# Attention tiles 0 to 7 of a two-layer kernel: exponentials per head, queries and keys loaded in 2 KB pieces and turned by products

## Chip, cores and metric

The kernel runs on one core of one Trainium2 chip. The metric is device time in microseconds (us) of one execution, the median of 3 runs. TensorE is called PE below, VectorE DVE, ScalarE ACT, GpSimd POOL and SyncE SP, as in the profile.

## What is computed

```python
def _attn_ref(q, k, v):                 # B, H, S, D = 8, 8, 576, 64; chunks of 64 tokens
    scores = scale * np.matmul(q_c, k_c.transpose(0, 1, 2, 4, 3))     # scale = 1/8
    scores = scores - np.max(scores, axis=-1, keepdims=True)
    attn = np.exp(scores)
    attn = attn / (np.sum(attn, axis=-1, keepdims=True) + 1e-09)
    return np.matmul(attn, v_c).reshape(B, H, S, D)

def reference(...):
    x = attn_out.transpose(0, 2, 1, 3).reshape(4608, 512)
    h = x @ w_in1;  g = np.maximum(h, 0.0) + alpha * np.minimum(h, 0.0);  x = g @ w_out1
    h = x @ w_in2;  g = h - np.tanh(h);                                  return g @ w_out2
```

Attention is within chunks of 64 tokens. q, k and v are float32; the weights (512x2048 and 2048x512 twice) and alpha are float64 and reach the chip as 64-bit words.

## The kernel before

The 4608 tokens are 36 tiles of 128 (two chunks, all 8 heads). Nine blocks of 512 tokens (4 tiles) go through layer 1, then through layer 2. A layer's hidden width of 2048 is walked in 16 pieces f of 128: `up` (L447) makes h of one f and 512 tokens with 12 products on PE, `act_g` (L461) applies the activation on ACT and DVE, `down` (L504) adds 12 products into four accumulators. Every float32 operand is held as a high and a low part, hence three products for one.

The program writes out the order of each engine's work itself: an engine runs its instructions in the order in which the functions are called. Tiles 0 to 3 are prepared before any step (L673 to L766). Tiles 4 to 7 are prepared inside steps 0 to 7 (`step_first`, L785), a step being one f of the first two blocks; while these run, the weights are converted from 64-bit words on ACT and DVE, one home d a step.

One tile's way, in the early form that the change touches:

- `load_natural` (L229) brings q and k of the tile, tokens on partitions: 1024 pieces of 256 bytes each, issued on SP.
- `att_a_early` (L280) turns q (i = 0) or k (i = 1) with four PE transposes of 128x128 into a PSUM tile (tr, trh) and copies it on ACT (on DVE for tile 0 and for k of tile 2) into qt or kt.
- `att_s_early` (L327) makes the scores, 16 products of 64x64, in PSUM: in `first_banks` for tiles 0 to 3, whose halves alternate (`first_banks[:, t % 2]`), in sc afterwards.
- `att_e` (L344) takes the maximum of each head's row on DVE (mx, L348), subtracts it there from all 512 columns into SBUF (p, L350), and takes the exponential of the whole tile on ACT (L353).
- `att_n` (L356) sums on DVE (sm, L359), adds 1e-9 (L361), inverts (rd, L362) and multiplies (L363, on POOL for tiles 0 to 2).
- `att_t_early` (L398) transposes p on PE (ptr) and copies it on ACT (pte or pt, L405); `att_v_early` (L407) multiplies with v (xpe or xp); `att_xh` and `att_xl` write the high part on ACT (xh, L435) and the low part on DVE (xl, L439).

`convert_a(d)` (L149) takes the raw words of weight home d apart on ACT (wm L113, wr L116), `convert_b(d, ops)` (L165) puts float32 together in four operations on DVE (ops 0 to 3: L126, L130, L132, L136), `split_w` (L183) makes the high part on ACT (L174) and the low part on DVE or POOL (L181). Homes s0 and s1 hold w_in pieces 0 and 1 of layer 1, home 0 the next two pieces; up(0) needs s0, up(1) needs s1. `warm(n)` puts n products of zeros on PE. In step 1 the transposes ptr of tile 4 stand ahead of up(1) on PE.

Of the kernel before, what the change touches and what calls it, by code (L numbers as in the profile page):

```python
# [27 lines left out]
def kernel(  # L28
# [136 lines left out]
    def convert_b(d, ops=(0, 1, 2, 3)):  # L165
        to_f32_b([w_parts[d]], ops)
# [113 lines left out]
    def att_a_early(t, i):  # L280

        if t < NPT + 2:
            tr = ps_y.tile([P, HP, P], F32, tag=f"y{i if t < NPT else 2 - 2 * (t % 2) + i}", name="tr")
        else:
            tr = ps_h.tile([P, HP, P], F32, tag="h", name="trh")
        for hp in range(HP):
            nc.tensor.transpose(tr[:, hp, :], raws[t][i][:, hp * P:(hp + 1) * P], ident)
        to = (qts, kts)[i][t].rearrange("p h c d -> p h (c d)")
        if t == 0 or (t, i) == (2, 1):
            nc.vector.tensor_copy(to, tr)  # L290
        else:
            nc.scalar.activation(out=to, in_=tr, func=AF.Copy)  # L292
# [48 lines left out]
                    )  # L341
        scs[t] = sc

    def att_e(t, early=False):  # L344
        scv = scs.pop(t)
        a, b = (HP, 2) if early else (2, HP)
        mx = stat.tile([P, a, b, 1], F32, tag="mx", name="mx")
        nc.vector.tensor_reduce(out=mx[:, :, :, 0], in_=scv, op=ALU.max, axis=AX.X)  # L348
        p = first_p[:, t] if t < NPT else att.tile([P, H, D], F32, tag="p", name="p")
        nc.vector.tensor_tensor(  # L350
            out=p.rearrange("p (a b) d -> p a b d", a=a), in0=scv, in1=mx.to_broadcast([P, a, b, D]), op=ALU.subtract
        )
        nc.scalar.activation(out=p, in_=p, func=AF.Exp, scale=scale)  # L353
        ps[t] = p

    def att_n(t, engine=nc.vector):  # L356
        p = ps[t]
        sm = stat.tile([P, H], F32, tag="sm", name="sm")
        nc.vector.tensor_reduce(out=sm, in_=p, op=ALU.add, axis=AX.X)  # L359
        rd = stat.tile([P, H, 1], F32, tag="rd", name="rd")  # L360
        nc.vector.tensor_scalar(out=sm, in0=sm, scalar1=1e-9, scalar2=None, op0=ALU.add)  # L361
        nc.vector.reciprocal(out=rd[:, :, 0], in_=sm)  # L362
        engine.tensor_tensor(out=p, in0=p, in1=rd.to_broadcast([P, H, D]), op=ALU.mult)  # L363
# [43 lines left out]
    def att_v_early(t):  # L407
        vt, pt = vts.pop(t), pts.pop(t)
        if t < NPT:
            xp = [ps_y.tile([P, HP, D], F32, tag=f"y{2 - 2 * (t % 2) + c}", name="xpe") for c in range(2)]  # L410
        else:
            both = new_banks("xp")[:, :, :HP * D].rearrange("p c (h d) -> p c h d", h=HP)
            xp = [both[:, c] for c in range(2)]
        for hp in range(HP):
            for e in range(2):
                for c in range(2):
                    r = slice(64 * c, 64 * c + 64)
                    nc.tensor.matmul(
                        out=xp[c][64 * e:64 * e + 64, hp, :],
                        lhsT=vt[r, 2 * hp + e, :],  # L420
                        rhs=pt[r, hp, 64 * e:64 * e + 64],
                        start=True,
                        stop=True,
                    )
        xps[t] = xp
# [239 lines left out]
            qts[t0 + t], kts[t0 + t] = qt[:, t], kt[:, t]  # L665

    def load_first(t):
        load_natural(t, first_raw[t // 2][:, t % 2])

    new_first(0)  # L670
    load_first(0)
# [3 lines left out]
    load_first(3)  # L675
    load_v(0)
    load_v(1)
    load_w("s1")
    load_v(2, first_v[:, 0])
    load_v(3, first_v[:, 1])  # L680
    arow = stage.tile([P, 512], F32, tag="st", name="arow")
    nc.sync.dma_start(out=arow[:KF, :P], in_=alpha.rearrange("(f p) -> f p", p=P))
    load_first(4)
    load_w(0)
    load_w(1)
    load_first(5)
    load_v(4, first_v[:, 2])
# [19 lines left out]
    att_a_early(1, 0)  # L707
    att_s_early(0)
    att_a_early(1, 1)
    att_e(0, True)  # L710
    warm(3)
    att_s_early(1)
    att_n(0, nc.gpsimd)
    convert_a("s0")
    att_a_early(2, 0)
    att_e(1, True)
    warm(4)
    att_a_early(2, 1)
    convert_b("s0", ops=(0, 1))
# [4 lines left out]
    convert_b("s0", ops=(2,))  # L724
    att_a_early(3, 0)
    att_a_early(3, 1)
    att_e(2, True)
    convert_b("s0", ops=(3,))
    warm(3)
    att_s_early(3)  # L730
# [54 lines left out]
    def step_first(step, j, t0, f, ends, x, acc):  # L785
# [133 lines left out]
```

## Time and profile before

| | |
|---|---|
| median of 3 runs | 1680.23 us (1678.89 to 1683.86) |
| the profiled execution | 1681.05 us |
| its span on the core | 1679.2 us |
| PE busy | 1651.2 us, 98% of the span |
| DVE, ACT, POOL busy | 1291.5, 817.0, 231.7 us |
| mean granted clock of PE | 0.996 |
| chain that ended last, by engine | PE 92%, DVE 3%, SP's queue 2%, DMA 1% |

How to read it: busy time is the sum of an engine's instructions. The chain that ended last is followed back from the last instruction, at each step to what released it. Windows give busy time in a stretch of the span, with the clock that PE was granted (1.00 is 2.4 GHz) and the share of time in which the DMA engines moved data. In a timeline a row is one or several like instructions with their start, their time, and the idle time of the engine before them with what ended it; a row "x32" of 16 products counts each float32 product twice.

### The profile page before, as it was taken

The page shows a single profiled execution, that of the slowest core. Times are in us where ns is not written, and L with a number is a line of the kernel's source. Part 1 is how long each engine was busy: PE and PEld are TensorE (multiplying, and loading weights), DVE is VectorE, ACT ScalarE, POOL GpSimd, SP SyncE. Part 2 cuts the span into 40 slices and gives each one's busy share as a digit, 9 for nine tenths or more (in the row PEclk, how much of TensorE's full clock was granted, in tenths as well). Part 3 has the DMA queues.
Part 4 walks back from the last instruction along what each step waited for, and adds up shares of the span by engine and source line. Part 5 has one row for each costly group of instructions (what it writes and reads, how often), then busy time and mean ns, then how long its engine had stood idle before and what let it go on. Part 6 is the DMA issues. An engine that isn't in the chain of part 4 may idle for free.

```text
span 1679.2 us, 24428 instructions
## 1 busy us (share of the span) xinstructions
PE 1651.2 (98%) x9405; PEld 1360.4 (81%) x9405; DVE 1291.5 (77%) x1864; ACT 817.0 (49%) x1465; POOL 231.7 (14%) x171
## 2 busy tenths in 40 slices
PE   7899999999999999999999999999999999999998
PEld 6688888888887888888887888888888888888886
DVE  7878855666666666564358989898989998999987
ACT  5756544454544454454445444444444444444443
POOL 1000000000000000000146222222222222222221
PEclk9999999999999999999999999999999999999999
DMA  9661424333333333431333010101010101010000
GB/s 228 192 188 40 114 52 100 95 95 86 90 84 102 87 90 70 101 95 39 113 100 114 1 51 1 51 0 51 0 51 1 51 1 51 1 41 10 20 7 26
DMA packets 215269, 112.77 MB, mean 67 GB/s; under 512 B 170592, under 2 KB 186992, under 8 KB 215152
## 3 DMA queue, kind: packets, MB, share of 16 engines
q1 hardware_dynamic: 215152, 111.20, 24.1%
q8 instruction: 74, 1.21, 0.3%
q14 instruction: 43, 0.35, 0.1%
HBM read 81.80 MB, written 29.36 MB: 66 GB/s over the span
## 4 chain that ended last, share of the span: by engine, by line
PE 92%; DVE 3%; SPq 2%; DMA 1%; issue 1%; ACT 1%; DVEq 0%; ACTq 0%
PE y L511 45%; PE hps L455 45%; PE sc L318 1%; SPq L224 1%; DVE g L501 1%; SPq L219 1%; PE sc L389 1%; DVE g L500 0%; DMA ysc<-yst 0%; DMA first<-in_k_dram 0%; SPq L99 0%; DVE g L498 0%; DVE wm L132 0%; PE tr L276 0%; DVE wm L136 0%
## 5 line engine op out<-in xcount | busy, mean ns | idle before, releaser
L455 PE MATMUL hps<-xh,w 128*128 128x512 f32 (+1 forms) x2312 | 573.3, 390 | 5.2 <-ACT kt L292 5.2
L455 PEld LDWEIGHTS hps<-xh,w 128*128 128x128 f32 x2312 | 434.2, 188 | 95.7 <-ACT kt L292 5.7
L455 PE MATMUL hps<-xl,w 128*128 128x512 f32 (+1 forms) x1156 | 309.0, 389 | 0.0
L511 PE MATMUL y<-ghi,w 128*128 128x512 f32 x1152 | 300.6, 394 | 2.7 <-ACT yst L531 2.7
L511 PE MATMUL y<-w,ghi 128*128 128x512 f32 x1152 | 293.9, 390 | 2.5 <-ACT ghi L481 2.5
L493 ACT ACTIVATE sq<-hps 128x512 f32<-128x512 f32 x144 | 86.1, 598 | 401.0 <-PE hps L455 400.5
L484 POOL TENSOR_TENSOR glo<-g,ghi 128x512 fp32r<-128x512 f32 x144 | 185.6, 1289 | 579.9 <-ACT ghi L481 579.9
L511 PEld LDWEIGHTS y<-w,ghi 128*128 128x128 f32 x1152 | 215.8, 188 | 49.0 <-ACT ghi L481 4.4
L455 PEld LDWEIGHTS hps<-xl,w 128*128 128x128 f32 x1156 | 217.5, 188 | 45.2
L511 PEld LDWEIGHTS y<-ghi,w 128*128 128x128 f32 x1152 | 213.1, 188 | 48.4 <-ACT yst L531 3.2
L469 DVE SCALAR_TENSOR_TENSOR g<-neg,nalpha_sb,g 128x512 f32<-128x512 f32 x144 | 107.4, 746 | 179.3 <-ACT g L468 179.3
L500 DVE SCALAR_TENSOR_TENSOR g<-w,g 128x512 f32<-128x512 f32 x144 | 243.4, 1690 | 0.0
L481 ACT ACTIVATE ghi<-g 128x512 fp32r<-128x512 f32 x288 | 181.5, 630 | 103.9 <-DVE g L469 86.1
L467 ACT ACTIVATE neg<-hps 128x512 f32<-128x512 f32 x144 | 85.9, 597 | 222.4 <-PE hps L455 220.9
L511 PE MATMUL y<-glo,w 128*128 128x512 f32 x576 | 164.7, 389 | 0.0
L511 PE MATMUL y<-w,glo 128*128 128x512 f32 x576 | 162.8, 389 | 0.0
L181 POOL TENSOR_TENSOR w<-wm,w 128x1024 fp32r<-128x1024 f32 (+1 forms) x18 | 42.2, 2346 | 840.5 <-ACT w L174 840.5
L484 DVE TENSOR_TENSOR glo<-g,ghi 128x512 fp32r<-128x512 f32 x144 | 108.2, 751 | 33.7 <-ACT ghi L481 32.9
L511 PEld LDWEIGHTS y<-w,glo 128*128 128x128 f32 x576 | 108.1, 188 | 22.9 <-DVE glo L484 0.4
L511 PEld LDWEIGHTS y<-glo,w 128*128 128x128 f32 x576 | 108.1, 188 | 22.4
L501 DVE SCALAR_TENSOR_TENSOR g<-sq,g 128x512 f32<-128x512 f32 x144 | 110.1, 764 | 5.0
L502 DVE COPY_PREDICATED g<-ktc,th 128x512 f32<-128x512 uint32 x144 | 108.5, 753 | 4.9
(95 smaller groups left out, 1384.0 us busy)
## 6 DMA issues: line engine op xcount, KB each, us to landing
yraw<-ysc SPq DMA_DIRECT2D x9, 1024.0 KB, 5.8
out_dram<-yst SPq DMA_DIRECT2D x36, 256.0 KB, 2.2
raww<-in_moe_w_in_dram SPq DMA_DIRECT2D x16, 512.0 KB, 6.3
v<-in_v_dram SPq DMA_DIRECT2D x32, 256.0 KB, 4.2
raww<-in_moe_w_out_dram SPq DMA_DIRECT2D x16, 512.0 KB, 6.0
rw<-in_moe_w_in_dram SPq DMA_DIRECT2D x16, 512.0 KB, 4.3
w<-mr SPq DMA_DIRECT2D x32, 256.0 KB, 2.1
rw<-in_moe_w_out_dram SPq DMA_DIRECT2D x16, 512.0 KB, 4.1
```

The lines of the kernel that those rows point to most:

```text
L181: lo_engine.tensor_tensor(out=w_[:, :, 1], in0=w, in1=w_[:, :, 0].bitcast(F32), op=ALU.subtract)
L219: nc.sync.dma_start(out=vt[off:off + n], in_=v[b, :, s:s + n, :].rearrange("h p d -> p h d"))
L455: nc.tensor.matmul(out=hp[:, cols], lhsT=w[:, a, m], rhs=x[b][:, kk, cols], start=(kk == 0 and i == 0), stop=(kk == KD - 1 and i == 2),)
L467: nc.scalar.activation(out=neg, in_=hp, func=AF.Relu, scale=-1.0)
L469: nc.vector.scalar_tensor_tensor(out=g, in0=neg, scalar=nalpha_sb[:, f:f + 1], in1=g, op0=ALU.mult, op1=ALU.add)
L481: nc.scalar.activation(out=hi, in_=g, func=AF.Copy)
L484: lo_engine.tensor_tensor(out=lo, in0=g, in1=hi.bitcast(F32), op=ALU.subtract)
L493: nc.scalar.activation(out=sq, in_=hp, func=AF.Square)
L500: nc.vector.scalar_tensor_tensor(out=g, in0=w, scalar=ce, in1=g, op0=ALU.add, op1=ALU.mult)
L501: nc.vector.scalar_tensor_tensor(out=g, in0=sq, scalar=ca, in1=g, op0=ALU.add, op1=ALU.mult)
L502: nc.vector.copy_predicated(g, mask, th)
L511: nc.tensor.matmul(out=acc[t], lhsT=lhsT, rhs=rhs, start=(f == ends[0] and i == 0), stop=(f == ends[1] and i == 2))
```

## The change

For tiles 0 to 3 and 5 to 7 (tile 4 spans two batches) q and k are loaded by `load_grouped`: a partition holds one head and one group of 8 consecutive tokens, one piece of 2 KB, so 128 pieces a load. `att_a_early` turns such a load with 16 products of 64x64 against the identity, whose results stand in PSUM by the token's place in its group; the copy to qt or kt puts tokens into order by its reading pattern. The heads of such a tile stand as 0 to 3 and 4 to 7 in the two halves of the partitions, and `att_v_early` picks its operand accordingly. Tile 4 keeps the old load and the transposes.

For tiles 0 to 7 `att_e` becomes `att_e_early`: DVE takes the maximum (L383) and multiplies its 128x8 numbers by -scale (L384); ACT then takes eight exponentials of 128x64 (L388), straight from the scores in PSUM, with the head's maximum as bias and the row sum as a second output. `att_n` finds these sums and leaves out its own.

The order changes with it. On SP the load of s1 goes behind v of tiles 2 and 3, and weights 0 go ahead of q and k of tile 4. The conversion of s1 goes behind the products with v of tile 3 (its last two operations behind xl of tile 3), and the turn of tile 4 behind up(0), inside step 0. In step 0 all four operations on the next weights come ahead of tile 4's maximum on DVE.

```diff
+    GT = 8
+    def grouped(t):
+        return t * P % S + P <= S
+    def load_grouped(t, raw):
+        b, s = divmod(t * P, S)
+        for i, src in enumerate((q, k)):
+            nc.sync.dma_start(out=raw[:, i], in_=src[b, :, s:s + P, :].rearrange("h (g j) d -> h g (j d)", j=GT))
+        raws[t] = raw[:, 0], raw[:, 1]
...
@@ att_a_early
-        for hp in range(HP):
-            nc.tensor.transpose(tr[:, hp, :], raws[t][i][:, hp * P:(hp + 1) * P], ident)
         to = (qts, kts)[i][t].rearrange("p h c d -> p h (c d)")
+        if grouped(t):
+            tr = tr.rearrange("p a b -> p (a b)").rearrange("p (j m) -> p j m", j=GT)
+            for j in range(GT):
+                for e in range(2):
+                    r = slice(D * e, D * e + D)
+                    nc.tensor.matmul(
+                        out=tr[r, j, :], lhsT=raws[t][i][r, j * D:(j + 1) * D], rhs=ident[r, r], start=True, stop=True
+                    )
+            tr, to = tr.rearrange("p j (m g) -> p m g j", m=H), to.rearrange("p h (c g j) -> p (h c) g j", c=2, j=GT)
+        else:
+            for hp in range(HP):
+                nc.tensor.transpose(tr[:, hp, :], raws[t][i][:, hp * P:(hp + 1) * P], ident)
...
+    def att_e_early(t):
+        scv = scs.pop(t).rearrange("p h c d -> p (h c) d")
+        mx = stat.tile([P, H], F32, tag="mx", name="mx")
+        nc.vector.tensor_reduce(out=mx, in_=scv, op=ALU.max, axis=AX.X)
+        nc.vector.tensor_scalar(out=mx, in0=mx, scalar1=-scale, scalar2=None, op0=ALU.mult)
+        ps[t] = p = first_p[:, t] if t < NPT else att.tile([P, H, D], F32, tag="p", name="p")
+        sums[t] = stat.tile([P, H], F32, tag="sm", name="sm")
+        for h in range(H):
+            nc.scalar.activation(
+                out=p[:, h, :], in_=scv[:, h, :], func=AF.Exp, scale=scale, bias=mx[:, h:h + 1],
+                accum_out=sums[t][:, h:h + 1],
+            )
...
     def att_n(t, engine=nc.vector):
         p = ps[t]
-        sm = stat.tile([P, H], F32, tag="sm", name="sm")
-        nc.vector.tensor_reduce(out=sm, in_=p, op=ALU.add, axis=AX.X)
+        sm = sums.pop(t, None)
+        if sm is None:
+            sm = stat.tile([P, H], F32, tag="sm", name="sm")
+            nc.vector.tensor_reduce(out=sm, in_=p, op=ALU.add, axis=AX.X)
...
@@ att_v_early
+                h = 2 * hp + e
+                half, slot = divmod(h, HP) if grouped(t) else (e, hp)
...
-                        rhs=pt[r, hp, 64 * e:64 * e + 64],
+                        rhs=pt[r, slot, 64 * half:64 * half + 64],
...
@@ loads
     load_v(1)
-    load_w("s1")
     load_v(2, first_v[:, 0])
     load_v(3, first_v[:, 1])
+    load_w("s1")
...
-    load_first(4)
     load_w(0)
+    load_first(4)
...
@@ before the steps
     att_v_early(1)
-    convert_a("s1")
     att_n(3)
...
     att_xh(2, x0, 2 * P)
-    convert_b("s1", ops=(0, 1))
     att_xl(2, x0, 2 * P)
     att_v_early(3)
+    convert_a("s1")
+    convert_b("s1", ops=(0, 1))
...
     att_xh(3, x0, 3 * P)
+    att_xl(3, x0, 3 * P)
     convert_b("s1", ops=(2, 3))
-    att_xl(3, x0, 3 * P)
     split_w("s1", nc.vector)
-    att_a_second(4)
...
@@ step_first
         if step == 0:
             hp = up(f, x, NB, slice(2 * P, NB), hp0)
+            att_a_second(t)
             att_s_early(t)
+            some((1, 2, 3))
         if even:
-            att_e(t, True)
-        some((1, 2))
+            att_e_early(t)
+        if step:
+            some((1, 2))
...
-        some((3,))
+        if step:
+            some((3,))
```

ACT's order up to the exponential of tile 4, before (in all these rows raww, wm and wr are raw words and parts of a weight home, 128x512 for s1 and 128x1024 for home 0; xpe is the product with v):

```order
L113 ACTIVATE wm<-raww 128x512
L116 ACTIVATE wr<-raww 128x512
L435 ACTIVATE xh<-xpe 128x4x64 x2
L405 ACTIVATE pte<-ptr 128x512
L435 ACTIVATE xh<-xpe 128x4x64 x4
L174 ACTIVATE w<-wm 128x512
L292 ACTIVATE qt<-tr 128x512
L292 ACTIVATE kt<-tr 128x512
L762 ACTIVATE nalpha_sb<-first 128x16
L113 ACTIVATE wm<-raww 128x1024
L116 ACTIVATE wr<-raww 128x1024
L353 ACTIVATE p<-p 128x512
```

and with the change:

```order
L444 ACTIVATE pte<-ptr 128x512
L476 ACTIVATE xh<-xpe 128x4x64 x2
L113 ACTIVATE wm<-raww 128x512
L116 ACTIVATE wr<-raww 128x512
L476 ACTIVATE xh<-xpe 128x4x64 x2
L174 ACTIVATE w<-wm 128x512
L802 ACTIVATE nalpha_sb<-first 128x16
L113 ACTIVATE wm<-raww 128x1024
L116 ACTIVATE wr<-raww 128x1024
L314 ACTIVATE qt<-tr 128x512
L314 ACTIVATE kt<-tr 128x512
L388 ACTIVATE p,sm<-sc,mx 128x64 x8
```

The exponential of 128x512 has become eight of 128x64. The words of s1 (wm, wr of 128x512) moved from between the parts xh of tiles 0 and 1 to behind those of tile 2, and the copies qt and kt of tile 4 from ahead of home 0's words to behind them.

DVE's order from the last operations on s1 to the product of tile 4, before:

```order
L136 ISA wm<-wm,wr 128x1024
L439 TENSOR_TENSOR xl<-xpe,xh 128x4x64 x2
L181 TENSOR_TENSOR w<-wm,w 128x512
L126 TENSOR_SCALAR wm<-wm 128x1024
L348 TENSOR_REDUCE mx<-sc 128x8
L350 TENSOR_TENSOR p<-sc,mx 128x512
L130 TENSOR_SCALAR wm<-wm 128x1024
L132 SCALAR_TENSOR_TENSOR wm<-raww,wm 128x1024
L359 TENSOR_REDUCE sm<-p 128x8
L361 TENSOR_SCALAR sm<-sm 128x8
L362 RECIPROCAL rd<-sm 128x8
L363 TENSOR_TENSOR p<-p,rd 128x512
```

and with the change:

```order
L132 SCALAR_TENSOR_TENSOR wm<-raww,wm 128x512
L136 ISA wm<-wm,wr 128x1024
L181 TENSOR_TENSOR w<-wm,w 128x512
L126 TENSOR_SCALAR wm<-wm 128x1024
L130 TENSOR_SCALAR wm<-wm 128x1024
L132 SCALAR_TENSOR_TENSOR wm<-raww,wm 128x1024
L136 ISA wm<-wm,wr 128x2048
L383 TENSOR_REDUCE mx<-sc 128x8
L384 TENSOR_SCALAR mx<-mx 128x8
L400 TENSOR_SCALAR sm<-sm 128x8
L401 RECIPROCAL rd<-sm 128x8
L402 TENSOR_TENSOR p<-p,rd 128x512
```

The subtraction (p<-sc,mx) and the sum (sm<-p) are gone, a scaling of mx has come. The four operations on home 0 (wm of 128x1024, the last of 128x2048) stand together ahead of tile 4's maximum; two of them stood inside the tile's chain and the last behind it.

## Rows read from the trace of the kernel before

**Rows 1.** Windows of the whole span and of 25 to 30 us; columns as named in the first row.
```profile
core 0: us, PE busy (x) PEld busy (x) DVE busy (x) ACT busy (x) POOL busy (x), PEclk, DMA share, GB/s
0.00:30.00 30.00, 25.76 (x385) 23.01 (x385) 19.69 (x43) 15.76 (x32) 5.37 (x10) 1.00 0.98 224
30.00:47.00 17.00, 9.17 (x111) 7.67 (x113) 14.66 (x21) 12.06 (x19) 0.00 (x0) 0.80 1.03 250
47.00:100.00 53.00, 46.81 (x369) 37.42 (x365) 44.60 (x64) 33.69 (x53) 0.00 (x0) 1.00 0.65 201
100.00:1679.00 1579.00, 1569.46 (x8549) 1292.29 (x8547) 1212.57 (x1738) 755.53 (x1365) 226.32 (x161) 1.00 0.21 58
...
25.00:30.00 5.00, 4.90 (x68) 4.47 (x65) 3.78 (x8) 3.46 (x10) 0.00 (x0) 1.00 0.94 308
```

**Rows 2.** Waits of PE in the first 50 us: total us, times, longest.
```profile
PE ptr L403 <- DVE p L363: 5.7, 1, 5.7
...
PE first L335 <- DVE p L350: 1.2, 2, 0.9
PE xpe L418 <- DVE xl L439: 1.1, 1, 1.1
...
PE tr L287 <- DMA first<-in_q_dram: 0.4, 1, 0.4
```

**Rows 3.** Timeline of PE, 7 to 37 us: start, us, instruction, idle before and releaser.
```profile
7.16 1.15 PE L335 MATMUL first<-kt,qt 64*64 64x64 f32 x32
...
9.92 1.15 PE L335 MATMUL first<-kt,qt 64*64 64x64 f32 x32 [0.36 <-DVE p L350]
...
14.96 1.09 PE L287 MATMUL tr<-ident,first 128*128 128x128 f32 x8
...
17.58 1.15 PE L335 MATMUL first<-kt,qt 64*64 64x64 f32 x32 [0.85 <-DVE p L350]
...
24.99 1.20 PE L455 MATMUL hps<-xh,w 128*128 128x256 f32 x8
...
29.27 0.63 PE L455 MATMUL hps<-xl,w 128*128 128x256 f32 x4
...
36.89 1.08 PE L403 MATMUL ptr<-ident,p 128*128 128x128 f32 x4 [5.66 <-DVE p L363]
```

**Rows 4.** Groups of ScalarE by shape: busy us, mean ns, idle before.
```profile
L481 ACT ACTIVATE ghi<-g 128x512 fp32r<-128x512 f32 x288 | 181.5, 630 | 103.9 <-DVE g L469 86.1 <-DVE g L502 17.9
L495 ACT ACTIVATE w<-sq,bias_sb 128x512 f32<-128x512 f32 x144 | 104.3, 724 | 0.0
...
L467 ACT ACTIVATE neg<-hps 128x512 f32<-128x512 f32 x144 | 85.9, 597 | 222.4 <-PE hps L455 220.9 <-ACT ptb L378 0.8
...
L762 ACT ACTIVATE nalpha_sb<-first 128x16 f32<-128x16 f32 x1 | 0.2, 186 | 0.0
```

**Rows 5.** Timeline of VectorE and ScalarE, 9 to 35 us.
```profile
9.08 0.69 DVE L350 TENSOR_TENSOR p<-first,mx 128x512 f32<-128x512 f32 x1
...
10.47 0.69 DVE L359 TENSOR_REDUCE sm<-p 128x8 f32<-128x512 f32 x1 [0.69 <-ACT p L353]
...
11.19 0.17 DVE L361 TENSOR_SCALAR sm<-sm 128x8 f32<-128x8 f32 x1
...
28.18 0.75 DVE L439 TENSOR_TENSOR xl<-xpe,xh 128x256 fp32r<-128x256 f32 x2
...
29.91 1.15 ACT L113 ACTIVATE wm<-raww 128x1024 f32<-128x1024 f32 x1
...
33.68 0.58 ACT L467 ACTIVATE neg<-hps 128x512 f32<-128x512 f32 x1
...
34.16 0.59 ACT L468 ACTIVATE g<-hps 128x512 f32<-128x512 f32 x1
```

**Rows 6.** Timeline of steps 2 and 3, 63 to 75 us.
```profile
63.67 1.15 PE L335 MATMUL sc<-kt,qt 64*64 64x64 f32 x32
...
69.21 0.69 DVE L363 TENSOR_TENSOR p<-p,rd 128x512 f32<-128x512 f32 x1
...
71.56 1.22 DVE L136 CUSTOM_DVE_ANT_0 wm<-wm,wr 128x2048 uint16<-128x2048 uint16 x1
...
74.49 0.73 PE L455 MATMUL hps<-xh,w 128*128 128x512 f32 x2 [2.64 <-ACT kt L292]
```

More of the change, by code (lines that the diff above doesn't have):

```diff
@@ L342, in att_s_early, with att_e @@
         scs[t] = sc
-    def att_e(t, early=False):
+    sums = {}
+    def att_e(t):
         scv = scs.pop(t)
-        a, b = (HP, 2) if early else (2, HP)
-        mx = stat.tile([P, a, b, 1], F32, tag="mx", name="mx")
+        mx = stat.tile([P, 2, HP, 1], F32, tag="mx", name="mx")
         nc.vector.tensor_reduce(out=mx[:, :, :, 0], in_=scv, op=ALU.max, axis=AX.X)
-        p = first_p[:, t] if t < NPT else att.tile([P, H, D], F32, tag="p", name="p")
+        p = att.tile([P, H, D], F32, tag="p", name="p")
         nc.vector.tensor_tensor(
-            out=p.rearrange("p (a b) d -> p a b d", a=a), in0=scv, in1=mx.to_broadcast([P, a, b, D]), op=ALU.subtract
+            out=p.rearrange("p (a b) d -> p a b d", a=2), in0=scv, in1=mx.to_broadcast([P, 2, HP, D]), op=ALU.subtract
         )
@@ L419, in att_v_early @@
                         out=xp[c][64 * e:64 * e + 64, hp, :],
-                        lhsT=vt[r, 2 * hp + e, :],
-                        rhs=pt[r, hp, 64 * e:64 * e + 64],
+                        lhsT=vt[r, h, :],
+                        rhs=pt[r, slot, 64 * half:64 * half + 64],
                         start=True,
@@ L667, in load_first @@
     def load_first(t):
-        load_natural(t, first_raw[t // 2][:, t % 2])
+        (load_grouped if grouped(t) else load_natural)(t, first_raw[t // 2][:, t % 2])
     new_first(0)
@@ L677 @@
     load_v(1)
-    load_w("s1")
     load_v(2, first_v[:, 0])
     load_v(3, first_v[:, 1])
+    load_w("s1")
     arow = stage.tile([P, 512], F32, tag="st", name="arow")
     nc.sync.dma_start(out=arow[:KF, :P], in_=alpha.rearrange("(f p) -> f p", p=P))
+    load_w(0)
     load_first(4)
-    load_w(0)
     load_w(1)
@@ L709 @@
     att_a_early(1, 1)
-    att_e(0, True)
+    att_e_early(0)
     warm(3)
@@ L715 @@
     att_a_early(2, 0)
-    att_e(1, True)
+    att_e_early(1)
     warm(4)
@@ L726 @@
     att_a_early(3, 1)
-    att_e(2, True)
+    att_e_early(2)
     convert_b("s0", ops=(3,))
@@ L735 @@
     att_v_early(0)
-    att_e(3, True)
+    att_e_early(3)
     att_t_early(2)
```

## Prediction

> **What bounds the kernel now.** I read the windows first [rows 1]. TensorE (PE) lacks 9.5 us in the 1579 behind 100 us, but 18.3 in the first 100: 4.2 up to 30 us, 7.8 from 30 to 47, 6.2 from 47 to 100. All that the change touches lies in those 100 us. What follows has no slack, so what the start gains or loses shows whole at the end.
>
> The waits of the first 50 us say who ends PE's idle time there [rows 2]: 5.7 us on VectorE's normalisation of tile 4, 1.2 on p, the subtraction of the tile before, 1.1 on xl; on a load only 0.4. So the start is a chain from engine to engine, although the DMA engines are busy all the time. The timeline gives its beat [rows 3]: the scores of tiles 0, 1 and 3 start at 7.16, 9.92 and 17.58, the first half of up(0) at 24.99; up(0) ends at 29.9, and the transposes of tile 4 (ptr), at the head of step 1, start at 36.89.
>
> One detail of these rows carries the forecast. The scores of tile 1 (9.92) and of tile 3 (17.58) are released by "DVE p L350", the subtraction of the tile before, though they write the other half of first_banks: the two halves are one tile to the dependency tracking. Whoever reads tile t's scores last releases the scores of t+1. Today that is a subtraction which ends 1.5 us behind the scores; with the change it is the last of eight exponentials.
>
> **The change part by part.**
>
> *Exponentials.* Per tile VectorE loses the subtraction (0.69) and the sum (0.69) and gains a scaling of 128x8, like the addition to sm (0.17) [rows 5]: 1.2 us less. ScalarE loses one exponential of 128x512 and gets eight of 128x64. Price of one: an activation of 128x512 out of PSUM takes 0.597, one of 128x16 takes 0.186, so 0.83 ns an element and 0.226 for 64. A bias that is read from memory costs 0.094 (724 against 630 ns) [rows 4]: 0.320. Two in a row overlap by 0.10 (33.68 for 0.58, the next at 34.16) [rows 5], so eight take 7 x 0.22 + 0.32 = 1.86 us. The row sum is a second result that no row here shows. Below: nothing, 1.86; were the bias free as well, 7 x 0.126 + 0.226 = 1.1. Above: a further shortest activation each, 8 x 0.186, makes 3.35. I take that shortest one with its overlap, 0.09 each: **E = 2.6 us**.
>
> *Turning.* Eight transposes occupy PE for 1.09, so four for 0.55; sixteen 64x64 products on two diagonal quarters, like the scores, 1.15 [rows 3]. So 0.6 more for each of 14 turns; bounds 0 and 0.6. The copies behind now read PSUM with a stride; they move as many elements, and I leave them at 0.6.
>
> *Loads.* Fourteen loads go from 1024 pieces of 256 bytes to 128 of 2 KB. On the path lies the 0.4 us of rows 2 and no more. The weights s1 go behind two loads of v, weights 0 ahead of tile 4; both are read after 30 us, issued 10 us before. The Trainium skill, DMA: Bandwidth & Descriptors, section "Specifications", gives 512 bytes as the least piece for full rate; by it the loads get faster, and the sum would be that of the second rival below.
>
> *Start.* The scores of tile 0 stand behind three turns: 3 x 0.6, less the 0.4 of load waits: **+1.4**.
>
> *Tiles 0 to 3.* On ScalarE the copy of a next turned k or q stands ahead of the exponentials. From scores to scores: scores 1.08, turn 1.08, copy 0.65, E 2.6, release 0.15 (9.77 to 9.92) make 5.55, twice; from tile 2 to 3 there are two turns, 6.6. In all 17.7 against 10.42 (7.16 to 17.58) [rows 3]: **+7.3**.
>
> *Scores of tile 3 to up(0).* Behind scores 1.1 and ptr(1) 0.6 ScalarE has pte(1) and the high part of s0, 0.6 each, so exponentials start 2.8 us on; then E; two small operations and the product 1.15; xl 0.75 [rows 5], release 0.15, products with v and ptr 1.2: 8.6 against 7.4: **+1.2**. The halves of up(0) keep their 4.9 us.
>
> *End of up(0) to ptr of tile 4.* The conversion of s1 moved behind xh(2), and the turn of tile 4 behind up(0) and, on ScalarE, behind weights 0. Counted from the end of up(0): xl of tile 3 ended 1.0 us earlier, the last two operations on s1 end at +0.45, its high part on ScalarE at +1.1, nalpha and two conversions of weights 0 (1.15 each [rows 5]) at +3.3, the copies qt and kt at +4.4, scores at +5.5. VectorE has the four operations on weights 0 ahead of the maximum (0.7, 0.7, 1.2, 1.2, from +2.35): until +6.1; maximum and scaling +7.0, E +9.6, normalisation +10.75, ptr **+10.9** against 7.0 (29.9 to 36.89): **+3.9**. Work that lay in the tile's gaps now lies ahead of it.
>
> *Steps 1 to 6.* Here VectorE is the beat: from scores (63.67) to the product (69.21), to wm (71.56), then kt on ScalarE and up at 74.49 [rows 6]. The exponentials can start 2.1 us behind the scores and end at 4.7, the sum is gone, and the product ends at 5.8 instead of 6.2: 0.4 for each of two turns of the loop, **-0.8**. The longer turns lie in PE's waits for kt.
>
> Sum: 1.4 + 7.3 + 1.2 + 3.9 - 0.8 = **+13.0 us**. The profiled execution took 1681.05, 0.8 above the median of 1680.23; 1681.05 + 13.0 - 0.8 gives **1693.2 us**. E enters five times in the first four terms and twice in the steps. E = 1.86: 13.0 - 3.7 - 1.5 = 7.8, or 1688.0. E = 3.35: 13.0 + 3.75 + 1.5 = 18.3, or 1698.5. PE's clock adds to the upper side: after the idle 5.66 us the window from 30 to 47 has 0.80 granted, a mixture of 2.4 and 1.2 GHz [rows 1]. The new gaps, 2.4 us in tiles 0 to 3, could do the same; five turns and scores on the path at half speed, 0.5 each, make 2.5 more, 1701.
>
> **The rivals.**
>
> *Cheap exponentials: no change.* If bias and sum cost nothing, E is 1.1: the first terms fall by 7.5, the steps gain the full 1.2 twice (1.6 more): +3.9, 1684.1. That is within 0.3% (5.0 us), about what a measurement of this kernel can tell from no change. The 0.094 of a bias in rows 4 speaks against it. Cheaper turns alone would take 0.6 on some six turns of the path: 3.6, 1689.6.
>
> *Loads set the beat: faster.* In the first 30 us the DMA engines are busy 0.98 of the time at 224 GB/s; between 25 and 30 us, where weights come, they move 308 [rows 1]. Seven tiles of 0.52 MB take 16.4 us at 224 and 11.9 at 308: 4.5 us earlier, and with the 1.2 of VectorE's work in one turn of the steps a gain of 5.7: 1674.5. It decides from where PE's waits end on loads; rows 2 give these 0.4 of 4.2 us, which speaks against it.
>
> *Half the DMA engines: slower still.* The new source has the 8 heads outermost, where the old one had 128 tokens. Should such a load spread over only 8 of the 16 engines, it moves at half of 224 GB/s: 2.34 us for 256 KB instead of 1.17. If q of tile 0 lands at 5.4, then k, q and k follow at 7.7, 10.1 and 12.4, and the chain starts some 3 us later than I have it: +16.0, 1696.2. No row of before shows a copy of this shape. The Trainium skill, DMA: Bandwidth & Descriptors, section "Why a DMA increments its semaphore by 16 and not by 1", states this rule: the number of engines is the largest up to 16 that divides the slowest dimension of both sides, here 8 and 128, so 8. By that rule the new loads get half the engines.
>
> **How the numbers follow.** Forecast (E from 1.5 to 3.4) 0.62; half the engines 0.15; cheap exponentials 0.15; loads set the beat 0.08. The first two are slower by over 5.0 us: 0.77. The third is within: 0.15. The last is faster: 0.08. The range goes from 1684 (cheap exponentials) to 1701 (E at its upper bound, and the clock); the faster case and a little above lie outside.
>
> **What would show it.** Right: the eight exponentials of tile 0 in 2 to 3.4 us; scores of tiles 0 to 3 about 5.5 to 6.6 us apart, released by ScalarE's p; up(0) starting near 34 us; ptr of tile 4 near 50, with PE idle before it; the part behind 100 us unchanged but for its place; VectorE with nearly 10 us less to do. Wrong: scores still 3 to 4 us apart (then E or the release is mis-sized), PE's waits ending on in_q or in_k (then the loads), or a delay that is won back between 47 and 100 us.

## The result, and the profile after

| | before | after |
|---|---|---|
| median of the runs beside each other | 1679.70 us (1678.89 to 1683.86, 4 runs) | 1694.46 us (1691.92 to 1697.11, 4 runs) |
| the profiled execution | 1681.05 us | 1691.92 us |
| PE, DVE, ACT busy | 1651.2, 1291.5, 817.0 us | 1658.5, 1283.7, 830.9 us |
| mean granted clock of PE | 0.996 | 0.997 |

The change makes the kernel slower: ratio 1.0083, 95% interval 1.0060 to 1.0106, 14.8 us. The forecast was 1693.2 us, within 1684 to 1701. A second measurement gave 1694.37 (in the experiments on the clock).

The windows of after answer to [rows 1]; the last one is longer because the span is.

```profile
core 0: us, PE busy (x) PEld busy (x) DVE busy (x) ACT busy (x) POOL busy (x), PEclk, DMA share, GB/s
0.00:30.00 30.00, 22.98 (x496) 20.98 (x500) 8.67 (x23) 14.77 (x65) 4.72 (x10) 1.00 0.74 194
30.00:47.00 17.00, 8.58 (x161) 7.37 (x151) 11.31 (x22) 10.39 (x35) 0.65 (x1) 0.95 0.95 231
47.00:100.00 53.00, 46.61 (x524) 37.09 (x525) 42.39 (x63) 44.26 (x114) 0.00 (x0) 0.92 0.59 166
100.00:1689.00 1589.00, 1580.37 (x8634) 1301.19 (x8632) 1221.37 (x1749) 761.48 (x1375) 227.07 (x161) 1.00 0.21 59
```

PE lacks 8.6 us in the last window, 9.5 before: the time is lost in the first 100 us, where it lacks 21.8 instead of 18.3. Its busy time has grown by 7.3 us as well, about what 14 turns of 1.15 us instead of some 0.6 add. The rows at half clock are the same in both profiles, ptr of tile 4 and the first products of up(1) behind it (1.09 and 3.76 us, before 1.08 and 3.76); they fall into the window from 47 to 100 us now (0.92), and fell into that from 30 to 47 before (0.80). In the first 30 us VectorE is busy for 8.67 us instead of 19.69, and the DMA engines are busy 0.74 of the time instead of 0.98.

The waits of PE in the first 50 us, against [rows 2], name the new chain: ScalarE's exponentials (L388) stand where VectorE's subtraction stood, and PE waits 1.6 us for loads instead of 0.4.

```profile
PE first L357 <- ACT p L388: 4.4, 2, 2.2
PE sc L357 <- ACT kt L314: 3.1, 1, 3.1
PE tr L304 <- DMA first<-in_q_dram: 1.6, 2, 0.9
PE first L738 <- ACT p L388: 1.4, 1, 1.4
```

The timeline of PE, against [rows 3], gives the time of each stage:

```profile
5.28 1.15 PE L304 MATMUL tr<-ident,first 64*64 64x64 f32 x32 [0.93 <-DMA first<-in_q_dram]
...
10.01 1.13 PE L357 MATMUL first<-kt,qt 64*64 64x64 f32 x32
...
15.12 1.15 PE L357 MATMUL first<-kt,qt 64*64 64x64 f32 x32 [2.19 <-ACT p L388]
...
20.34 1.15 PE L357 MATMUL first<-kt,qt 64*64 64x64 f32 x32
...
26.41 1.15 PE L357 MATMUL first<-kt,qt 64*64 64x64 f32 x32 [2.19 <-ACT p L388]
...
34.65 1.21 PE L496 MATMUL hps<-xh,w 128*128 128x256 f32 x8
...
38.86 0.64 PE L496 MATMUL hps<-xl,w 128*128 128x256 f32 x4
...
43.46 1.15 PE L357 MATMUL sc<-kt,qt 64*64 64x64 f32 x32 [3.08 <-ACT kt L314]
50.17 1.09 PE L442 MATMUL ptr<-ident,p 128*128 128x128 f32 x4 [5.57 <-DVE p L402]
...
122.02 1.03 PE L288 MATMUL tr<-ident,rawn 128*128 128x128 f32 x8
```

The last row is the turn of tile 8, the first behind the tiles that the change touches. Before it was this one:

```profile
109.08 1.03 PE L276 MATMUL tr<-ident,rawn 128*128 128x128 f32 x8
```

| stage | before | after | difference | forecast |
|---|---|---|---|---|
| scores of tile 0 start | 7.16 | 10.01 | +2.85 | +1.4 |
| scores of tile 0 to those of tile 3 | 10.42 | 16.40 | +5.98 | +7.3 |
| scores of tile 3 to up(0) | 7.41 | 8.24 | +0.83 | +1.2 |
| up(0) | 4.91 | 4.85 | -0.06 | 0 |
| end of up(0) to ptr of tile 4 | 6.99 | 10.67 | +3.68 | +3.9 |
| ptr of tile 4 to the turn of tile 8 (109.08, now 122.02) | 72.19 | 71.85 | -0.34 | -0.8 |
| sum | | | **+12.94** | +13.0 |

The two spans differ by only 10.6, because what follows varies: from the turn of tile 8 to the end it is 1570.1 us in this profile of before, 1567.8 in that of after, and between 1566.3 and 1569.7 in all those below, which do the same work there.

ScalarE's timeline shows the exponentials of tile 0. Each is followed by a row of its own that reads out the row sum; there are eight such pairs.

```profile
12.11 0.60 ACT L314 ACTIVATE kt<-tr 128x512 f32<-128x512 f32 x1 [1.27 <-PE tr L304]
12.61 0.31 ACT L388 ACTIVATE p<-first,mx 128x64 f32<-128x64 f32 x1
12.80 0.20 ACT L388 ACTIVATION_READ_ACCUMULATOR p<-first,mx 128x1 f32 x1
12.89 0.31 ACT L388 ACTIVATE p<-first,mx 128x64 f32<-128x64 f32 x1
...
14.82 0.25 ACT L388 ACTIVATION_READ_ACCUMULATOR p<-first,mx 128x1 f32 x1
```

A pair takes 0.29 us (12.61 to 12.89), eight take 2.46 (12.61 to 15.07): the E of the forecast, put at 2.6 between 1.1 and 3.35. The scores of tile 1 start 0.05 behind them.

### The profile page after: what moved, and what is told of

It is laid out like the page before. It is cut to its first block, busy times and chain, and to the rows that moved or that the text cites. A ratio compares the mean times of both kernels' runs of the same rounds, so it can differ in the third digit from the quotient of the medians.

```text
span 1689.8 us, 25330 instructions
## 1 busy us (share of the span) xinstructions
PE 1658.5 (98%) x9797; PEld 1366.6 (81%) x9797; DVE 1283.7 (76%) x1856; ACT 830.9 (49%) x1585; POOL 232.4 (14%) x171
## 3 DMA queue, kind: packets, MB, share of 16 engines
q8 instruction: 77, 1.26, 0.3%
## 4 chain that ended last, share of the span: by engine, by line
PE 92%; DVE 3%; SPq 2%; DMA 2%; ACT 1%; issue 1%; ACTq 0%; DVEq 0%
PE y L552 45%; PE hps L496 44%; PE sc L340 1%; DVE g L542 1%; PE sc L428 1%; SPq L219 1%; DMA first<-in_k_dram 1%; ACT p L388 1%; DVE g L541 0%; DMA ysc<-yst 0%; DMA first<-in_q_dram 0%; SPq L224 0%; SPq L243 0%; DVE g L539 0%; PE tr L288 0%
```

## The experiments

The theory is the forecast's sum: eight exponentials that release the next scores, dearer turns and later loads at the start, and work moved ahead of tile 4. There are twelve runs, one of them of the changed kernel once more; "the changed kernel" stands for 1694.4 us below.

### Three parts undone, each alone

**The old exponentials in the changed kernel.**

```diff
@@ att_e_early
-        nc.vector.tensor_scalar(out=mx, in0=mx, scalar1=-scale, scalar2=None, op0=ALU.mult)
...
-        for h in range(H):
-            nc.scalar.activation(out=p[:, h, :], in_=scv[:, h, :], func=AF.Exp, scale=scale, bias=mx[:, h:h + 1], ...
+        nc.vector.tensor_tensor(out=p..., in0=scv, in1=mx.to_broadcast([P, HP, 2, D]), op=ALU.subtract)
+        nc.scalar.activation(out=p, in_=p, func=AF.Exp, scale=scale)
```

> The changed kernel, but tiles 0 to 7 take their exponentials in the old way (subtraction and sum on VectorE, one exponential of 128x512 on ScalarE). Theory (the eight exponentials of tile t, 2.46 us, release the scores of t+1): the scores of tiles 0 to 3 come 3 to 4 us apart again, 10.5 to 11.5 us in all instead of 16.4, released by VectorE's p; steps 2 to 7 lose some 0.5; 5.5 us less than the changed kernel, about 1689. Rival (the later loads and the dearer turns set this loop): the scores stay 5 us or more apart and the time falls by less than 1.5, 1693 or more.

Measured: 1688.99 us (1687.43 to 1690.27), ratio to before 1.0051, 1.0036 to 1.0065. PE's timeline has the scores without a wait:

```profile
11.00 1.10 PE L357 MATMUL first<-kt,qt 64*64 64x64 f32 x32
...
13.83 1.15 PE L357 MATMUL first<-kt,qt 64*64 64x64 f32 x32
...
19.66 1.15 PE L357 MATMUL first<-kt,qt 64*64 64x64 f32 x32
...
23.46 1.15 PE L357 MATMUL first<-kt,qt 64*64 64x64 f32 x32
```

12.46 us for the loop instead of 16.40; 5.4 us less in all. (The first two turns ran at half clock here, 1.97 us each, so the scores of tile 0 start at 11.00.) That the middle step still takes 5.83 was not expected; PE is busy in all but 0.35 us of it, and two of the dearer turns stand in it. The rival falls for the greater part: without the eight exponentials no wait holds this loop, but at 12.46 it stays 2.0 above the 10.42 of before, with the turns still in it.

**The old loads and transposes.**

```diff
     def grouped(t):
-        return t * P % S + P <= S
+        return False
```

> The changed kernel, but q and k of all tiles 0 to 7 come by the old load (1024 pieces of 256 bytes) and are turned by four transposes of 128x128. Theory (later loads and dearer turns cost the start, and each turn on the path 0.6): the first turn waits 0.4 instead of 0.93 us, the wait of 0.66 before the second goes, the scores of tile 0 start near 7.2 instead of 10.0, their loop takes 1 to 2 us less; 4 us less than the changed kernel, about 1690.5. Rival (the exponentials and the order make nearly all of it, ScalarE takes up any earlier start): less than 1.5 us, 1693 or more. A second rival (the 2 KB loads help, by the DMA engines' time that they leave to others): slower than the changed kernel, 1697 or more.

Measured: 1689.84 us (1686.94 to 1691.15), ratio 1.0054, 1.0039 to 1.0069; 4.5 less. The scores of tile 0 start at 7.27, their loop takes 15.59 us, 0.8 less, and PE still waits 2.38 and 2.43 us for ScalarE's p in it:

```profile
7.27 1.15 PE L357 MATMUL first<-kt,qt 64*64 64x64 f32 x32
...
22.86 1.71 PE L357 MATMUL first<-kt,qt 64*64 64x64 f32 x32 [2.43 <-ACT p L388]
```

The profiled execution is the slowest of the four (1691.15 us, mean clock 0.992). Against the first profile of the changed kernel (0.997) ptr of tile 4 is only 2.4 earlier (47.73); against the second (below), whose clock of 0.993 is like this one's, it is 6.9 earlier, and the span is 4.4 shorter (1689.0 against 1693.4).

**The old order.**

```diff
     load_v(1)
+    load_w("s1")
...
     att_v_early(1)
+    convert_a("s1")
...
     split_w("s1", nc.vector)
+    att_a_second(4)
...
@@ step_first
-            att_a_second(t)
             att_s_early(t)
-            some((1, 2, 3))
```

> The changed kernel with the order of before: on SP s1 ahead of v of tiles 2 and 3 and tile 4 ahead of weights 0, the conversion of s1 among the tiles, the turn of tile 4 ahead of step 0's conversion, and on VectorE tile 4's maximum behind the first operation on weights 0. Theory (work that lay in the gaps of the tiles now lies ahead of tile 4): from the end of up(0) to ptr of tile 4 it takes some 7.9 us instead of 10.67, all before it stays as it was, and the time falls by 2.5, about 1692. Rival (the conversion of s1 among the tiles delays ScalarE's exponentials, so what is won behind up(0) is lost ahead of it): up(0) starts 1 us or more later than 34.65 and the time stays within 1 us of 1694.5.

Measured: 1689.66 us (1687.91 to 1690.43), ratio 1.0053, 1.0036 to 1.0070; 4.7 less. The end of the chain in PE's timeline:

```profile
37.90 1.82 PE L496 MATMUL hps<-xh,w 128*128 128x256 f32 x8
...
42.78 0.64 PE L496 MATMUL hps<-xl,w 128*128 128x256 f32 x4
...
49.52 1.09 PE L442 MATMUL ptr<-ident,p 128*128 128x128 f32 x4 [5.02 <-DVE p L402]
```

From the end of up(0) (43.42) to ptr it takes 6.10 us instead of 10.67, 4.6 less, where 2.8 less were expected. up(0) does start 3.25 later than in the first profile of the changed kernel, as the rival has it, but not by its mechanism: the second profile of the changed kernel, which also ran a stretch of this part at half clock (below), takes 9.60 us from the scores of tile 3 to up(0), and this run 9.67. No delay by the conversion of s1 among the tiles shows in these rows.

The three differences, 5.4, 4.5 and 4.7, add up to 14.6, the whole loss. Each ratio is known to some 0.15%, 2.5 us, so that the sum fits this well may be chance.

### What holds the scores of tile t+1

**A PSUM tile of their own for the scores of tiles 1 and 3.**

```diff
-        bank = first_banks[:, t % 2] if t < NPT else new_banks("sc")[:, 0]
+        bank = (ps_y.tile([P, 512], F32, tag="y2", name="odd") if t % 2 else first_banks[:, 0]) if t < NPT else new_banks("sc")[:, 0]
...
-            xp = [ps_y.tile([P, HP, D], F32, tag=f"y{2 - 2 * (t % 2) + c}", name="xpe") for c in range(2)]
+            xp = [ps_y.tile([P, HP, D], F32, tag=f"y{2 * (t % 2) + c}", name="xpe") for c in range(2)]
```

> The changed kernel, but the scores of tiles 1 and 3 stand in a PSUM tile of their own (the products with v of even and odd tiles swap theirs), so they do not wait for the readers of the tile before. Theory (release of one common tile by the last exponential): scores of tile 1 start near 12.5 instead of 15.12, without a wait for ScalarE's p, tile 3 some 3 us earlier than 26.41; up(0) starts 3 us or more earlier than 34.65; about 1691. Rival (ScalarE's own queue of copies, exponentials and the words of s0 is the beat, the release only shows it): the scores of tile 1 come earlier but the exponentials of tile 1 start within 0.5 us of where they did, up(0) within 1 us; 1693.5 or more.

Measured: 1690.92 us (1690.47 to 1691.77), ratio 1.0063, 1.0048 to 1.0078; 3.5 less. The scores start at 11.27 (the first two turns ran at half clock again), 14.09, 19.31 and 23.12, without a wait: 11.85 us against 16.40. The common tile is what held them. But up(0) starts 22.14 us behind the first scores instead of 24.64, so of 4.55 us 2.05 go again. The waits of PE show where:

```profile
PE xpe L459 <- ACT p L388: 1.9, 1, 1.9
PE ptr L442 <- POOL p L402: 1.4, 1, 1.4
```

The first is the price of the swap (the product with v of tile 1 now stands behind tile 3's exponentials), the second POOL's normalisation; ptr of tile 3 ran at half clock besides (1.11 us). The rival is half right: ScalarE is the next limit. It works without a gap from 13.84 us, the first exponential of tile 0, to 20.9.

**The exponentials alone, in the kernel before** (att_e_early and the sums of att_n, nothing else).

> The kernel before with the eight exponentials alone (all tiles 0 to 7; old loads, transposes and order). Theory (they cost the loop of tiles 0 to 3 what the run with the old exponentials gave back): scores of tiles 1 to 3 again 5 us or more apart, released by ScalarE's p; from the end of up(0) to ptr of tile 4 about 6.1 us instead of 6.99, as in the run with the old order; about 5.5 slower than before, 1685.5. Rival (the costs do not add, they share one chain: with the old loads or order the exponentials hide): less than 2 us slower, under 1682.

Measured: 1685.64 us (1682.81 to 1689.96, 10 runs), ratio 1.0031, 1.0019 to 1.0044; 5.7 slower than before, as much as their removal gave back. The scores of tiles 0 to 3 take 15.59 us (7.46 to 23.05); from the end of up(0) (38.25) to ptr of tile 4 (44.33) it takes 6.08 instead of 6.99. For tile 4 the exponentials are a gain, for tiles 0 to 3 a loss.

### The price of the second result

```diff
-            nc.scalar.activation(..., bias=mx[:, h:h + 1], accum_out=sums[t][:, h:h + 1])
+            nc.scalar.activation(..., bias=mx[:, h:h + 1])
```

> The changed kernel without the second result of the exponentials (VectorE sums the rows again, 0.69 us a tile). Theory (the read of the accumulator, 0.20 to 0.25 us in a row of its own, is what makes a pair take 0.29): the rows of that read are gone, eight exponentials take 1.7 to 1.9 us instead of 2.46, the scores of tiles 1 and 3 come some 0.6 earlier behind those of the tile before; the sum on VectorE takes part of it back; 1 to 2 less than the changed kernel, about 1693. Rival (the reads overlap with the next exponential, the read of the bias or of PSUM sets the spacing): eight take 2.3 us or more, and with the sum on VectorE the time is the same or up to 1 slower, 1694.5 to 1695.5.

Measured: 1691.45 us (1691.23 to 1692.09), ratio 1.0062, 1.0042 to 1.0082; 2.9 less. ScalarE's timeline, eight exponentials in a row:

```profile
12.08 0.60 ACT L314 ACTIVATE kt<-tr 128x512 f32<-128x512 f32 x1 [1.29 <-PE tr L304]
12.58 1.74 ACT L387 ACTIVATE p<-first,mx 128x64 f32<-128x64 f32 x8
```

1.74 us instead of 2.46, and the waits for p are 1.46 and 1.47 instead of 2.19. So a read of the accumulator costs 0.09 us, 0.72 a tile, and leaving VectorE's sum of 0.69 in place is cheaper. The rival falls.

### Half the DMA engines

**Token groups outermost in the new loads.** The halves of the partitions are then the two chunks, so `att_v_early` takes another half of its operands, and v comes in four loads.

```diff
-            nc.sync.dma_start(out=raw[:, i], in_=src[b, :, s:s + P, :].rearrange("h (g j) d -> h g (j d)", j=GT))
+            nc.sync.dma_start(out=raw[:, i], in_=src[b, :, s:s + P, :].rearrange("h (g j) d -> g h (j d)", j=GT))
```

> The changed kernel with the token groups outermost in the new loads (16 groups of 8 heads instead of 8 heads of 16 groups, pieces of 2 KB as before; the two halves of the partitions are then the two chunks, and v of these tiles comes in four loads by head parity and chunk instead of one, issued on SP behind q and k). Theory (a load whose outermost dimension is 8 moves on half of the 16 DMA engines): the DMA share in 2 to 4 us rises from 0.39 to 0.7 or more, the first turn starts by 4.6 instead of 5.28, the wait of 0.66 before the third turn goes, scores of tile 0 start near 8.6 instead of 10.0; 1 to 1.5 less than the changed kernel if the four loads of v hide, about 1693. Rival (the 2 KB pieces themselves, or their issue on SP, 0.6 us each, set the landing): share below 0.5 and the first turn after 5.1.

Windows of the changed kernel, 2 to 6 us:

```profile
2.00:4.00 2.00, 2.00 (x12) 2.00 (x10) 0.00 (x0) 0.02 (x1) 0.00 (x0) 1.00 0.39 100
4.00:6.00 2.00, 1.07 (x26) 0.86 (x27) 0.00 (x0) 0.00 (x0) 0.00 (x0) 1.00 0.65 228
```

and of this run:

```profile
2.00:4.00 2.00, 2.00 (x12) 2.00 (x10) 0.00 (x0) 0.01 (x1) 0.00 (x0) 1.00 0.88 227
4.00:6.00 2.00, 1.85 (x29) 1.58 (x30) 0.00 (x0) 0.00 (x0) 0.00 (x0) 1.00 0.99 227
```

The same pieces of 2 KB move at 227 GB/s with a share of 0.88, where they moved at 100 with 0.39; SP's issues take 0.6 us each as they did, so the rival falls. The old pieces of 256 bytes had moved as fast in this stretch of the kernel before:

```profile
2.00:4.00 2.00, 2.00 (x12) 2.00 (x10) 0.00 (x0) 0.01 (x1) 0.00 (x0) 1.00 1.07 234
```

The first turn starts at 4.55, nothing waits for a load, the scores of tile 0 start at 9.27 although the first turn ran at half clock (1.89 us instead of 1.15). The rule that the Trainium skill, DMA: Bandwidth & Descriptors, section "Why a DMA increments its semaphore by 16 and not by 1", gives for the number of engines agrees with this: 8 for the loads of the change, 16 here.

Time: 1693.86 us (1693.44 to 1695.02), ratio 1.0077, 1.0059 to 1.0094, no difference to the changed kernel that can be told: from the scores of tile 3 to up(0) it takes 9.15 us (8.24), behind a ptr of 1.12 us at half clock, and the products with v have become dearer by the edit. Rows of this run's PE timeline, the start and such a product:

```profile
4.55 1.89 PE L314 MATMUL tr<-ident,first 64*64 64x64 f32 x32
...
9.27 1.10 PE L367 MATMUL first<-kt,qt 64*64 64x64 f32 x32
...
36.42 1.20 PE L469 MATMUL xpe<-pte,v 64*64 64x64 f32 x32
```

In the changed kernel they take 0.69 us at the same clock. There the program spreads the sixteen over all four quarters of PE's rows and columns, here over the two diagonal ones, as in the scores (1.15). Tile 8 is turned at 123.28, 1.26 later than in the first profile of the changed kernel, though the scores of tile 0 were 0.74 earlier. So the price of the half engines is read from the start alone; the time of this run does not give it.

### Where the runs differ: the clock

**The changed kernel once more.**

> The changed kernel once more, unchanged, for a second profile and more runs. Theory (half clock behind the new gaps comes in some executions and not in others): the median lies between 1692 and 1695, the runs order themselves by their mean granted clock, and where the profile has a mean clock below 0.997 its first 50 us show stretches at half clock that the first profile did not have, about as long as the difference. Rival (the spread has another source): runs with the same clock differ by 2 us or more.

Measured: 1694.37 us (1691.18 to 1697.64, 5 runs), ratio 1.0084, 1.0070 to 1.0098. The profiled run took 1695.52 with a mean clock of 0.993. Its windows, the first two against 1.00 and 0.83 in the first profile:

```profile
0.00:30.00 30.00, 23.86 (x431) 22.01 (x431) 7.81 (x21) 12.99 (x57) 3.64 (x9) 0.94 0.76 196
30.00:60.00 30.00, 20.07 (x228) 17.31 (x227) 18.62 (x34) 19.28 (x59) 1.73 (x2) 0.67 0.93 230
```

and rows of its PE timeline:

```profile
15.97 1.93 PE L357 MATMUL first<-kt,qt 64*64 64x64 f32 x32 [2.21 <-ACT p L388]
17.68 1.92 PE L304 MATMUL tr<-ident,first 64*64 64x64 f32 x32
...
28.81 1.25 PE L357 MATMUL first<-kt,qt 64*64 64x64 f32 x32 [2.20 <-ACT p L388]
30.00 1.11 PE L442 MATMUL ptr<-ident,p 128*128 128x128 f32 x4
...
38.41 1.88 PE L496 MATMUL hps<-xh,w 128*128 128x256 f32 x8
...
54.60 1.09 PE L442 MATMUL ptr<-ident,p 128*128 128x128 f32 x4 [4.83 <-DVE p L402]
```

Behind the two new waits of 2.2 us, turns and scores take 1.9 us instead of 1.15 and ptr 1.11 instead of 0.66: 1.2 GHz for a while, where the first profile kept 2.4 behind the same waits. ptr of tile 4 starts at 54.60 instead of 50.17, the turn of tile 8 at 126.83 instead of 122.02: 4.8 us, in stages that hold rows at half clock and no new wait (the first two turns among them, 1.97 and 1.83 us, which put the scores of tile 0 at 10.86). The runs go with their clocks, though not strictly: 1691.18 (0.996), 1693.02 (0.997), 1694.37 (0.994), 1695.52 and 1697.64 (both 0.993), so 2 us between runs have another source.

**Products of zeros in three gaps of the changed kernel.** They compute nothing that is read.

```diff
     att_e_early(0)
-    warm(3)
+    warm(13)
...
     convert_b("s0", ops=(3,))
-    warm(3)
+    warm(13)
...
             att_s_early(t)
+            warm(24, rest)
             some((1, 2, 3))
```

> The changed kernel with products of zeros in three of its gaps: ten more ahead of the scores of tile 1 and of tile 3 (0.18 us each, 1.8 of the 2.19), 24 behind the scores of tile 4 (4.3 of the 5.57). They compute nothing that is read. Theory (behind a gap the engine is granted 1.2 GHz for a while, which is why runs with a mean clock of 0.992 to 0.994 are 2 to 5 us longer than the one of 0.997): the granted clock stays 1.00 from 40 to 60 us, the first products of up(1) take 2.1 us for eight instead of 3.76, the runs spread by less than 2 us and the median falls by 2.5 to 4, to 1690.5 to 1692. Rival (the clock after a gap does not depend on such products, or they delay what stands behind them): no gain, 1694 or more.

Measured: 1690.57 us (1689.03 to 1693.06, 5 runs), ratio 1.0062, 1.0049 to 1.0074; 3.8 less, with mean clocks of 0.996 to 0.999. Window and spread were missed: the runs spread by 4.0 us, and the clock from 40 to 50 us is 0.66. The gap of 3.07 us ahead of the scores of tile 4 had not been filled; they and the 24 products ran at half clock and pushed ptr of tile 4 to 52.68. up(1) then ran at 2.4 GHz, and the scores of tile 5 start at 60.20, where they did (60.12). So what is gained can only come from the two gaps among tiles 0 to 3: up(0) starts at 34.53, as in the first profile of the changed kernel (34.65) and 3.9 ahead of the second (38.41), where half clock followed these gaps. No run parts it further.

**The same 24 products in the kernel before.**

> The kernel before with 24 products of zeros behind the scores of tile 4 and nothing else. Theory (the clock behind the gap costs 2.2 us): granted clock 1.00 from 37 to 43 us instead of 0.50 to 0.64, 1677.5 to 1678.5. Rival: within 0.7 us of before, 1679.2 or more.

Measured: 1679.30 us (1677.53 to 1680.26, 11 runs), ratio 0.9993, 0.9984 to 1.0001. The timeline of PE:

```profile
31.50 5.63 PE L697 MATMUL rest<-zero 128*128 128x128 f32 x48
37.12 0.66 PE L403 MATMUL ptr<-ident,p 128*128 128x128 f32 x4
...
40.39 1.03 PE L287 MATMUL tr<-ident,first 128*128 128x128 f32 x8
...
45.84 1.98 PE L335 MATMUL sc<-kt,qt 64*64 64x64 f32 x32 [3.79 <-DVE xl L439]
```

ptr takes 0.66 instead of 1.08, and the turn of tile 5 starts at 40.39 instead of 42.57: 2.2 us, as expected. But the scores of tile 5 wait 3.79 us for VectorE's xl instead of 2.09 and start 0.5 earlier, now themselves at half clock, and so do the products of up(2) behind them (3.78 us for eight instead of 2.14). Most of what the half clock had cost lay beside VectorE's work, and the longer wait was followed by a half clock of its own. The rival holds.

### What beats both kernels

**The exponentials where they gain (tiles 4 to 7) and the split banks, in the kernel before.**

> The kernel before with the eight exponentials for tiles 4 to 7 alone, and the scores of tiles 1 and 3 in a PSUM tile of their own. Theory: two waits for VectorE's p (0.36 and 0.85) go, from the end of up(0) to ptr of tile 4 it takes 6.1 us instead of 6.99, steps 2 to 7 gain 0.4; 1.5 to 2.5 less than before, about 1678. Rival (what is won in tiles 0 to 3 is taken by POOL's normalisation or the conversion of s0, and only the tail of 1 us shows): within 1 us of before.

Measured: 1679.68 us (1676.59 to 1681.87, 12 runs), ratio 0.9994, 0.9984 to 1.0003: within 1 us of before, as the rival has it. Both waits for p are gone and the scores of tile 3 start 0.74 earlier (16.84), but up(0) only 0.2 (24.79): PE waits 1.1 us for POOL's normalisation instead of 0.3. ptr of tile 4 starts 0.6 earlier (36.27) and the scores of tile 5 1.2 (45.09), but those of tile 6 0.2 later (63.86). Here the rival named no cause: up ran at half clock behind a wait for kt:

```profile
55.79 2.52 PE L473 MATMUL hps<-xh,w 128*128 128x512 f32 x8 [2.52 <-ACT kt L292]
58.11 1.91 PE L473 MATMUL hps<-xl,w 128*128 128x512 f32 x4
```

The profile of before has a like wait, of 2.59, and 1.08 for the second row.

**That, with the 24 products behind the scores of tile 4.**

> The run of before with the eight exponentials for tiles 4 to 7 and the split banks, and 24 products of zeros behind the scores of tile 4. Theory (the half clock behind that gap costs ptr 0.4 and the first twelve products of up(1) some 1.8): 2 us less than without them, 1677 to 1678, and 2 to 3 less than before. Rival: the products push ptr of tile 4 back, or the clock falls elsewhere: 1679.5 or more.

Measured: 1676.85 us (1675.80 to 1677.79, 11 runs), ratio 0.9981, 0.9972 to 0.9990: 2.9 less than before, every run at a mean clock of 0.997 or 0.998. The scores of tile 5 start at 44.85, those of tile 6 at 61.83 (63.67 before), the turn of tile 8 at 108.07 (109.08). 1.0 us of the gain against before stands in these rows, and 2.0 against the run without the 24 products, whose turn of tile 8 starts at 110.04; the rest of the 2.9 is not located. In the same measurement the runs of before lie between 1677.71 and 1682.88.

## Why the prediction was right

The two large terms came by the mechanism that was named: 5.98 us for the 7.3 of tiles 0 to 3, 3.68 for the 3.9 of tile 4. That their sum is met within 0.1 is luck: the start was put 1.45 too low, the tiles 1.3, the way to up(0) 0.4 and that to tile 4 0.2 too high, the steps 0.5 too good, and these cancel.

- **The bound** (the start is a chain, nothing is won back behind it): right. The delay of 13.28 us at ptr of tile 4 is still 12.94 at the turn of tile 8.
- **Exponentials, E = 2.6**: 2.46. The parts were nearly those of the working: 1.74 without the row sum (1.86 put), and 0.09 for each read of it (0.09 put, chosen between nothing and 0.186 without a row to show it).
- **Tiles 0 to 3, +7.3**: +5.98, the mechanism right (both waits "<-ACT p L388", and gone with a tile of their own). The steps of 5.55, 5.55 and 6.6 were 5.11, 5.22 and 6.07: E was 0.14 too long, and the exponentials start 2.60 us behind the scores (10.01 to 12.61), not 2.81.
- **Scores of tile 3 to up(0), +1.2**: +0.83.
- **End of up(0) to ptr of tile 4, +3.9**: +3.68. The two runs with the old order (6.10 and 6.08) show the parts: the moved work costs 4.6, the exponentials give back 0.9.
- **Start, +1.4**: the step that failed. It took three turns at 0.6 and no load on the path; measured are +2.85. With the loads on all engines the scores of tile 0 come at 8.5 (9.27 less the 0.74 of a turn at half clock), that is +1.4, as worked out; the other 1.45 is the rival "half the DMA engines", which was held at 0.15 and is what happens. Its price was set too high (+3 us): q and k landed early enough to leave waits of 0.93 and 0.66 only.
- **Steps, -0.8**: -0.34. The waits for kt did fall, to 0.89 and 0.66 us from 2.59 and 2.64, but the longer turns, which the working put at nothing because they lie in these waits, use up 1.1 of each (two turns of 1.15 us instead of 0.60). Of the two turns of the loop one gained 0.39, as forecast, the other 0.07 (16.96 and 17.28 us from scores to scores, 17.35 before). The way from ptr of tile 4 to the scores of tile 5, which the working left out, costs 0.5 (9.95 against 9.43): the turns of tile 5 there take 2.02 us instead of 1.03.
- **The clock**, put only into the upper end: it is in most executions (six of nine have a mean clock of 0.992 to 0.994). The sum of +13.0 meets a run that kept its clock up to ptr of tile 4 (+12.94 at the turn of tile 8); the medians, 14.7 higher, hold executions like the second profile, which has 4.8 us more there.
- The rival "cheap exponentials" falls with E, 2.46 and not 1.1. "Loads set the beat" falls with the result and with the run that has the old loads and turns, 4.5 us faster than the changed kernel; the larger pieces move no faster even on all engines (227 against 234 GB/s).
- VectorE was to have nearly 10 us less to do: the rows that went and came make 9.5, its busy time fell by 7.8 (1291.5 to 1283.7), as other rows vary.

## What to carry to other kernels

Ask who reads a PSUM tile last before the next stage may write into it: an operation that is dearer there costs its whole length once a tile, even where its engine is idle half the time and another engine is relieved. One fused instruction instead of two can be the slower one when it is cut into eight and moved to an engine in the chain, and the same edit pays where something else hides it (tile 4). Look at the outermost dimension of a load as well as at the size of its pieces, and compare runs at a like clock before a microsecond or two is given a cause.

## What the hardware showed that was not expected

- The row sum of an activation is read by an instruction of its own, 0.19 to 0.25 us in the trace, of which 0.09 show in the distance of two exponentials (0.29 with it, 0.20 without).
- 2 KB pieces with 8 heads outermost moved at 100 GB/s from 2 to 4 us, the same pieces with 16 groups outermost at 227, and 256-byte pieces with 128 tokens outermost at 234.
- A wait of 2.2 us on PE was followed by half clock in one execution and by full clock in another of the same program (turns and scores of 1.9 and of 1.15 us behind it).
- Sixteen 64x64 products with v took 0.69 us on four quarters of PE and 1.20 on two diagonal ones.
